# Pooled rows spread over the value blocks, weight sums on two engines, and a planner that counts a shared port

## The chip, the cores and the metric

The kernel runs on one core of one Trainium2 chip, in one launch. The metric is device time in microseconds. A run's time is that of the whole execution; a profile gives the span from the first to the last instruction, and a little time lies around it.

## The reference, cut to what matters

Eight batches, eight heads, 576 positions, 64 values a head, all in float32. Two attentions are added: one over rows averaged by fours, and one over a window of three neighbours on each side. A token mixer and a channel mixer follow, each of two matrix products with a ReLU between and a sum with its input.

```python
q_d, k_d, v_d = (t.reshape(B, H, S // 4, 4, D).mean(axis=3) for t in (q, k, v))
out_up = np.repeat(softmax(scale * q_d @ k_d.T) @ v_d, 4, axis=2)          # pooled
mask = np.abs(pos[:, None] - pos[None, :]) < 4
out_local = softmax(np.where(mask, scale * q @ k.T, -1e9)) @ v             # windowed
x = (out_up + out_local) as (B, S, H * D)                                  # 576 x 512 a batch
h = relu(x.transpose(0, 2, 1) @ w_tok1) @ w_tok2                           # 576 -> 256 -> 576
u = x + h.transpose(0, 2, 1)
out = u + relu(u @ w_ch1) @ w_ch2                                          # 512 -> 1536 -> 512
```

## The kernel before, in words

**Attention.** `load` brings queries and keys of one batch (`qk`, four tiles of 579 KB). `pool_q` sums them by fours into `qd`, on VectorE (DVE) for batches 0 and 1 and on GpSimd (POOL) later; `load_v` and `later_v` do the same for the values (`vr` into `vd`). `pooled` runs the pooled attention, one pair of heads a step: scores `sd`, maximum, exponential, transposes `td`, product `ad` with `vd`, and the scaled result `od`. `local` runs the windowed attention by tiles of four blocks of 32 queries (the last tile has two): scores `sc` against a window of `WB` keys, mask, maximum, exponential and scaling in the tile `P`, transposes `pT`, and the product `av` with the value blocks `vw`. A value block has, on 64 partitions for each head of a pair, one row of zeros, the 38 rows of the window and then 8 rows (39 to 46) for the pooled results of its 32 positions. So one product adds both attentions: columns 39 to 46 of `P` hold a constant pattern `rep` that repeats each pooled row four times, and column 0 holds the softmax's epsilon. `load_w` fills the window rows of `vw` with four DMAs a batch; once the last pair of `pooled` is done, two DMAs store `od` into the pooled rows, from ACT's queue in batches 0 and 1 and from SP's in the others.

**Mixers.** `mix` holds the token mixer. The channel mixer of batches 0 and 1 is plain (`first`, `second`, products `c` with the weights `CW` and `CX`). From batch 2 on it is a Strassen-like scheme of seven products (`first_blocks`, `second_blocks`, products `cx`, `cy`, `cz`, `dX`, `dY`, `dZ`), with chains of small additions in `after` on ACT, DVE and POOL. Its weights are sums of blocks of the weights. `weight_sums` makes them once, on POOL: six groups for each of the two weights (`C1`, then `C2`), each of four sums that are written as a high half and a rest (`put`). `keep` stores each result to HBM at once by SP's queue, and `fetch` loads them back as units `wa`, `wb`, `wc_*` for every batch.

**What sets the order.** Nothing is ordered by hand. Each piece of work is a generator that yields `step(engine, us, needs, ...)`, and `drive` is a list scheduler that runs while the kernel is built: it keeps a clock for each engine, takes the step that can start first, and among those within `PATIENCE` on the same engine the one that stands first in the list of streams. The instructions of a step are emitted then, and each engine and queue takes its instructions in that order. So the planned durations decide the order, and the real ones the time. `fetched` plans a DMA's landing from a clock `D` and a rate; `in_turn` lets at most three weight loads be under way. Until the first channel product, `keep_busy` fills planned idle time of PE with products of a constant tile `junk`.

Of the kernel before, what the change touches and what calls it, by code (L numbers as in the profile page):

```python
# [6 lines left out]
F32 = mybir.dt.float32  # L7
# [13 lines left out]
WB = QB + 6  # L21
KB = 1 + WB + QB // 4
# [9 lines left out]
BIASED = range(2, 8)  # L32
HOP = 0.12
TURN = 0.1
# [5 lines left out]
def tile_ups_attention_mixer(ctx, tc, qk, vw, vr, w1, w2, c1, c2, out):  # L40
# [15 lines left out]
    def open_pool(k, name, side):  # L56
        if k in opened:
# [6 lines left out]
    HOME = dict(cw="B", h="B", SG="B", h7="B", f="B", uh0="A", uh1="A", wy="A", ra="A", rb="A", uh="A")  # L64
    psum = ctx.enter_context(tc.tile_pool(name="psum", bufs=1, space=bass.MemoryType.PSUM))
    BUFS = dict(cw=6, h=5, xh=3, x=4, u=8, uh0=4, uh1=4, qk=4, qd=1, vw=1, vd=1, pt=2, od=1, sm=12, ev=8, sc=24,
                SG=6, wy=4, ra=3, rb=3, uh=7, h7=6)
# [28 lines left out]
    junk = pools["B"].tile([128, 512], BF16, name="junk")  # L96
# [23 lines left out]
    for p in PT:  # L120
        nc.vector.memset(p, 0.0)
        nc.vector.memset(p[:, :, 0:1], EPS)
        nc.vector.tensor_copy(p[:, :, 1 + WB:KB], rep.unsqueeze(1).to_broadcast([128, H, QB // 4]))

# [15 lines left out]
    clock = dict(A=2.0, G=5.0, V=2.0, P=0.0, S=0.0, D=0.0, R=0.0)  # L140
# [5 lines left out]
    def step(engine, us, *needs, at=None, take="", give="", mode=None):  # L146
        return engine, us, needs, at, take.split(), give.split(), mode
# [6 lines left out]

    def fetched(nbytes, rate=350e3):
        clock["D"] = max(clock["D"], now[0]) + nbytes / rate
        return clock["D"] + 1.7

    def keep_busy(n):

        if n:
            ps = P1("busy")
            for _ in range(n):
                nc.tensor.matmul(ps, junk[:, :128], junk, start=True, stop=True)

    def drive(streams):
# [3 lines left out]
        while True:  # L170
# [4 lines left out]
            for it in items:  # L175
                e, us, needs, at, take, give, m = it[1]
                if not may(it[1]) or any(not free[k.split('>')[0]] for k in take):
                    continue
                t = max([clock[e], it[2] if at is None else at] + [made[n] for n in needs]
                        + [min(free[k.split('>')[0]].values()) for k in take])  # L180
                some.append((t + (TURN if e == "P" and m != mode else 0.0), t, it))
# [3 lines left out]
            e, us, _, _, take, give, m = it[1]  # L185
# [10 lines left out]
            clock[e] = t + us  # L196
            it[2] = t + us + HOP
# [8 lines left out]
    def to_f32(raw, at, y=None, *needs):  # L206
# [9 lines left out]
        e = yield step("V", 0.08 + n * 0.0012, *needs)  # L216
# [20 lines left out]
    def token_weight(i, n, f):  # L237
        yield step("A", 0.0, ("W", "raw", i))
        raw = made["W", "raw"][i]
        if i < len(TILES):  # L240
            y = WY[i] = T([f.shape[0], n], F32, "SG", f"W1_y{i}")
        else:
            y = WY[i]
# [4 lines left out]
    def token_split(i, n, f):  # L248
        yield step("A", 0.1 + n * 0.0011, ("W", "y", i), ("t1", 0, i) if i < len(TILES) else ("mixed", 0))
        nc.scalar.copy(f[:, 0], WY[i])  # L250
        e = yield step("V", 0.08 + n * 0.0012)
# [15 lines left out]
    class Channel:  # L267
# [31 lines left out]
        def parts(self, i):  # L299
# [4 lines left out]
            t = yield step("V", 0.75)  # L304
# [102 lines left out]
    def load_v(st):  # L407
# [17 lines left out]
        for i in range(8):  # L425
# [4 lines left out]
            e = yield step("G", 1.25, at=arrives[i])  # L430
            nc.gpsimd.tensor_add(t[:, 0:2], t[:, 0:2], t[:, 2:4])
            nc.gpsimd.tensor_add(st.vd[:, g, 2 * pr:2 * pr + 2, :D], t[:, 0].rearrange("p (h d) -> p h d", d=D),
# [3 lines left out]
    def later_v(st, g):  # L436
# [5 lines left out]
        for pr in range(4):  # L442
# [4 lines left out]
            e = yield step("G", 1.3, at=fetched(147e3, 230e3), give="w")  # L447
            nc.gpsimd.tensor_add(t[:, 0:2], t[:, 0:2], t[:, 2:4])
            nc.gpsimd.tensor_add(st.vd[:, g, 2 * pr:2 * pr + 2, :D], t[:, 0].rearrange("p (h d) -> p h d", d=D),
# [3 lines left out]
    def load_w(st):  # L453
        st.vw = T([128, HG, 2, 256], F32, "vw", f"vw{st.b}")
        for lo_, hi_ in ((0, 5), (5, HG)):
            for par in range(2):
                nc.sync.dma_start(st.vw[64 * par:64 * par + 1 + WB, lo_:hi_].rearrange("p g h c -> p (g h c)"),
                                  vw[st.b, par, :, 512 * lo_:512 * hi_])
        make(("vw", st.b), fetched(1.4e6, 152e3))

    def pool_q(st, hp):
        wide = st.b < 2
        e = yield step("V" if wide else "G", 1.62 if wide else 2.9, at=st.at[hp])
        if hp == 0:
            st.qd = T([128, 4, 2, Sd], F32, "qd", f"qd{st.b}")
# [3 lines left out]
        if wide:  # L469
            for h in range(2):  # L470
                o = st.qd[:, hp, 0, G * h:G * h + G].rearrange("p (r g) -> p r g", g=HG)
                nc.vector.tensor_reduce(o, q[:, h], axis=AX.X, op=ALU.add)
            nc.vector.tensor_reduce(st.qd[:, hp, 1], k, axis=AX.X, op=ALU.add)
        else:
            o = st.qd[:, hp, 0].rearrange("p (h r g) -> p h r g", h=2, g=HG)
            for to, x in ((o, [q[:, :, :, :, f] for f in range(4)]), (st.qd[:, hp, 1], [k[:, :, f] for f in range(4)])):
                nc.gpsimd.tensor_add(to, x[0], x[1])  # L477
                nc.gpsimd.tensor_add(to, to, x[2])
                nc.gpsimd.tensor_add(to, to, x[3])
# [5 lines left out]
    def pooled(st, pr):  # L485
# [60 lines left out]
        if pr == 3:  # L546
            e = yield step("A" if b < 2 else "S", 0.2, ("vw", b), *(("pair", b, i) for i in range(3)), at=e)
            for par in range(2):
                (nc.scalar if b < 2 else nc.sync).dma_start(
                    st.vw[64 * par + 1 + WB:64 * par + KB].rearrange("p g h c -> p g (h c)"),  # L550
# [3 lines left out]
    def local(st, t):  # L554
# [18 lines left out]
        w = pp[:n, :, 1:1 + WB]  # L573
        mask = masks[0 if t == 0 else 2 if t == len(TILES) - 1 else 1]
        yield step("V", 1.48, give="gg")
        nc.vector.tensor_tensor(w.rearrange("p (hp two) k -> p two hp k", two=2),
                                ps[:n, :, :4 * WB].rearrange("p two (hp k) -> p two hp k", hp=4),
                                mask[:n].unsqueeze(1).unsqueeze(1).to_broadcast([n, 2, 4, WB]), ALU.add)
        mx = T([n, H], F32, "sm", f"mx{b}_{t}")
        nc.vector.tensor_reduce(mx, w, axis=AX.X, op=ALU.max)  # L580
        nc.vector.tensor_tensor(w, w, mx.unsqueeze(2).to_broadcast([n, H, WB]), ALU.subtract)
        yield step("A", 0.47)
        nc.scalar.activation(w, w, AF.Exp, scale=0.125)
        yield step("V", 1.16)
# [3 lines left out]
        nc.vector.tensor_tensor(w, w, r.unsqueeze(2).to_broadcast([n, H, WB]), ALU.mult)  # L588
# [13 lines left out]
        for hp in range(4):  # L602
            for j in range(nb):
                h, g = divmod(TILES[t][j], HG)
                for par in range(2):
                    p = slice(64 * par, 64 * par + KB)
# [25 lines left out]
    def mix(st):  # L632
# [8 lines left out]
        def splits():  # L641
            for t in range(NT if b else 0):
# [4 lines left out]
                e = yield step("V", 0.75)  # L647
# [89 lines left out]
        def scaled():  # L737
            for ch in range(2):
# [8 lines left out]
                for c in range(4):  # L747
# [3 lines left out]
                    e = yield step("V", 0.5)  # L751
# [4 lines left out]
        def combined():  # L756
# [9 lines left out]
            def split(name):  # L766
# [4 lines left out]
                e = yield step("V", 1.0)  # L771
                for k in range(2):
                    nc.vector.scalar_tensor_tensor(t[:, k, 1], block[name][k], s, t[:, k, 0], ALU.mult, ALU.subtract)
                make(("uh", b, name), e)

            def less(x, y, name, into=None):
# [3 lines left out]
                for k in range(2):  # L780
                    e = yield step("V", 0.5, at=0.0 if k else None, take="" if into or b == 2 else f"f>{name}{k}_{b}")
# [107 lines left out]
    def weight_sums():  # L889

        add, sub = ALU.add, ALU.subtract
        t = pools["B"].tile([128, 2, 256], F32, name="S_sum")
        eng = nc.gpsimd

        def keep(C, p, name, x):
            if C is C1:
                to, i = {"A11": (A_UNITS, 0), "S1": (A_UNITS, 1), "S2": (A_UNITS, 2), "S4": (A_UNITS, 3),
                         "A12": (B_UNITS, 0), "S3": (B_UNITS, 1), "A22": (B_UNITS, 2)}[name]
                nc.sync.dma_start(to[p][:, i], x)
            else:  # L900
                for o in range(2):
                    nc.sync.dma_start(C_UNITS[o][name][:, p], x[:, o] if name[0] == "S" else x[:, :, 128 * o:128 * o + 128])

        def put(C, p, name, x):
            yield step("G", 0.5)
            if C is C1:
                out_ = T([128, 2, 256], F16, "SG", f"{name}_{p}")
                hi, lo = out_[:, 0], out_[:, 1]
            else:
                out_ = T([128, 2, 2, 128], F16, "SG", f"{name}_{p}")  # L910
                hi, lo = out_[:, :, 0], out_[:, :, 1]
                x = x.rearrange("p (o n) -> p o n", o=2)
            if C is C2 and name == "S1":
                eng.tensor_scalar(hi, x, -1.0, None, ALU.mult)
                yield step("G", 1.2)
                eng.tensor_tensor(lo, x, hi, add)
                eng.tensor_scalar(lo, lo, -1.0, None, ALU.mult)
            else:
                eng.tensor_copy(hi, x)
                yield step("G", 0.75)  # L920
# [419 lines left out]
```

## Time and profile before

| | us |
|---|---|
| median of three runs (lowest to highest) | 928.46 (927.17 to 929.52) |
| profiled execution, its own time | 928.45 |
| its span | 926.7 |
| PE busy (share of the span) | 858.6 (93%) |
| PE weight loads busy | 679.7 (73%) |
| DVE busy | 617.0 (67%) |
| ACT busy | 410.5 (44%) |
| POOL busy | 463.2 (50%) |

PE is TensorE's products and PEld its weight loads, which run beside them; DVE is VectorE, ACT ScalarE, POOL GpSimd, and SP the engine from whose queue nearly all DMAs are issued (SPq and ACTq mark issues). `L607` is line 607 of the kernel. `out<-in` names tiles without buffer numbers, and a shape like `47*32 47x64` is that of a product. In a timeline each row has a start, a duration, the instructions that were merged (`x4`), and in brackets the idle time of the engine before them with what ended it. That last name is inferred: where the engine it names had long been done, something else ended the wait.

### The profile page before, as it was taken

The numbers are of one execution on the slowest core, as the hardware profiler recorded it, in microseconds if no ns is written. First come the engines' busy times: TensorE is split into PE (matmuls) and PEld (weight loads), VectorE is DVE, ScalarE is ACT, GpSimd is POOL, SyncE is SP. The second block draws the span as 40 slices with busy tenths as digits, with TensorE's granted clock in tenths as the row PEclk, the third lists the DMA queues.
The fourth block names the chain that finished last, engine by engine and source line by source line (L and its number), as shares of the span: only waits on it lengthen the run. The fifth ranks groups of instructions, "written<-read, shape, count | busy, mean of one in ns | idle before, by whom it ended". The sixth has DMA issues, their size and how long they took to land. (4 is left out here: it accounts for less than half of the span.)

```text
span 926.7 us, 26502 instructions
## 1 busy us (share of the span) xinstructions
PE 858.6 (93%) x11020; PEld 679.7 (73%) x11024; DVE 617.0 (67%) x1347; ACT 410.5 (44%) x958; POOL 463.2 (50%) x676
## 2 busy tenths in 40 slices
PE   8498997999599999999989999899998999999998
PEld 4355776788478877878768786778767787787776
DVE  7758996447433757688477775778475885765662
ACT  3256552324233436554365435554254544652540
POOL 6227899789969914950197205850077401330340
PEclk9889999899899999999999999999999999999999
DMA  8885336633354318544774367644565445336653
GB/s 246 223 289 191 109 95 152 200 85 87 77 172 105 95 54 290 155 148 144 216 197 139 104 168 247 162 133 129 160 216 131 145 152 145 112 103 210 200 171 120
DMA packets 71015, 145.43 MB, mean 157 GB/s; under 512 B 16720, under 2 KB 32592, under 8 KB 69648
## 3 DMA queue, kind: packets, MB, share of 16 engines
q1 hardware_dynamic: 70576, 143.16, 51.1%
q8 instruction: 86, 1.41, 0.6%
q10 hardware_dynamic: 320, 0.59, 0.3%
q14 instruction: 33, 0.27, 0.1%
HBM read 120.91 MB, written 20.45 MB: 153 GB/s over the span
## 5 line engine op out<-in xcount | busy, mean ns | idle before, releaser
L1060 POOL TENSOR_TENSOR h<-t,h 128x288 f16<-128x288 f32 x108 | 83.2, 776 | 185.8 <-ACT h L1049 175.9
L987 PEld LDWEIGHTS <-wa 128*128 128x128 f16 x864 | 81.9, 98 | 30.0 <-issue 7.8
L1148 PEld LDWEIGHTS <-wc_S 128*128 128x128 f16 x864 | 84.2, 99 | 22.0
L127 PE MATMUL c<-uh,CW 128*128 128x288 f16 x576 | 77.0, 289 | 1.4 <-DVE h L851 1.1
L987 PEld LDWEIGHTS <-wb 128*128 128x128 f16 x648 | 62.3, 98 | 19.5 <-issue 3.3
L127 PE MATMUL c<-h,CX 128*128 128x288 f16 x576 | 75.5, 287 | 0.0
L1148 PEld LDWEIGHTS <-wc_A 128*128 128x128 f16 x648 | 62.6, 98 | 16.4 <-issue 0.8
L127 PE MATMUL t<-xh,W 128*128 128x512 f32 x210 | 60.7, 422 | 11.5 <-DVE xh L648 8.7
L477 POOL TENSOR_TENSOR qd<-qk 128x144 f32<-128x144 f32 x48 | 30.9, 644 | 76.0 <-DMA qk<-in_qk_dram 76.0
L127 PEld LDWEIGHTS <-CW 128*128 128x128 f16 x576 | 55.6, 99 | 16.9 <-issue 2.5
L127 PEld LDWEIGHTS <-CX 128*128 128x128 f16 x576 | 55.0, 98 | 14.9 <-issue 1.1
L987 PE MATMUL cx<-uh_T,wb 128*128 128x288 f16 x432 | 64.8, 286 | 1.1 <-DVE y L1091 1.1
L1148 PE MATMUL dX<-h,wc_S 128*128 128x288 f16 x432 | 59.6, 294 | 0.0
L127 PE MATMUL t<-W,hid 128*128 128x288 f32 x336 | 58.4, 309 | 0.0
L1049 ACT ACTIVATE h<-t 128x288 f16<-128x288 f32 x108 | 47.9, 443 | 22.6 <-DVE t L1064 22.5
L607 PE MATMUL av<-vw,pt 47*32 47x64 f32 x2304 | 34.5, 241 | 25.0 <-DMA vw<-od 14.5
L1148 PE MATMUL dY<-h,wc_S 128*128 128x288 f16 x432 | 56.9, 286 | 0.0
L1148 PE MATMUL dX<-h,wc_A 128*128 128x288 f16 x432 | 56.6, 286 | 0.0
L127 PEld LDWEIGHTS t<-xh,W 128*128 128x128 f32 x210 | 38.1, 192 | 23.4 <-DVE xh L648 12.0
L607 PEld LDWEIGHTS av<-vw,pt 47*32 47x32 f32 x2304 | 28.1, 113 | 34.3 <-issue 24.0
L770 ACT ACTIVATE uh_T<-T,us 128x288 f16<-128x288 f32 x48 | 23.8, 529 | 59.5 <-DVE T L784 59.5
L648 DVE TENSOR_TENSOR xh<-x,xh 128x512 fp32r<-128x512 f32 x28 | 21.5, 774 | 41.0 <-ACT xh L646 40.9
(191 smaller groups left out, 2034.2 us busy)
## 6 DMA issues: line engine op xcount, KB each, us to landing
qk<-in_qk_dram SPq DMA_DIRECT2D x32, 579.0 KB
wa<-d1a SPq DMA_DIRECT2D x36, 512.0 KB
wc_S<-d_S SPq DMA_DIRECT2D x48, 384.0 KB
wb<-d1b SPq DMA_DIRECT2D x36, 384.0 KB
wc_A<-d_A SPq DMA_DIRECT2D x36, 384.0 KB
vr<-in_vr_dram SPq DMA_DIRECT2D x64, 144.0 KB
C_raw<-in_c_dram SPq DMA_DIRECT2D x16, 512.0 KB
out_dram<-u SPq DMA_DIRECT2D x24, 288.0 KB
```

Source lines behind the costliest of these rows:

```text
L127: nc.tensor.matmul(ps, lhs(a), rhs(c), start=first and i == 0, stop=last and i == 2, **kw)
L477: nc.gpsimd.tensor_add(to, x[0], x[1])
L607: nc.tensor.matmul(ps[QB * j:QB * j + QB, par, D * hp:D * hp + D], pt[p, hp, QB * j:QB * j + QB], st.vw[p, g, h, D * hp:D * hp + D], start ...
L648: nc.vector.tensor_tensor(xh[:, 1], xf(t), xh[:, 0].bitcast(F32), ALU.subtract)
L770: nc.scalar.activation(t[:, k, 0], block[name][k], AF.Copy, scale=s)
L987: nc.tensor.matmul(ps, w[:, a, 128 * k:128 * k + 128], uh[x][:, k, c], start=first_ and k == j == 0, stop=k == 1 and j == 2, skip_group_ch ...
L1049: nc.scalar.activation(here().h[:, PARTS.index(name), 0], x, f)
L1060: nc.gpsimd.tensor_tensor(h[:, i, 1], getattr(here(), x), h[:, i, 0], ALU.subtract)
L1148: nc.tensor.matmul(ps, w[:, k, a], H[k][:, i, c], start=first_ and k == j == 0, stop=k == 5 and j == 2, skip_group_check=True)
```

## The change

It has these parts:

- The window is 40 keys wide instead of 38. A value block is now loaded whole, 64 partitions for each head, in two DMAs a batch instead of four. The pooled rows lie at partitions 3, 10, 17, ... 52 of a block, with five window rows between each two. `P` has the matching columns in groups of seven, and the softmax operations work on 8 x 5 columns of a head.
- `od` is stored from SP's queue in all batches.
- `weight_sums` exists twice, once for POOL and once for DVE; each takes the next group that nobody has. On DVE, the high halves are made by ACT. The stores are steps of their own (`stores`) that become due 3 us (POOL) or 1.5 us (DVE) after the planned time of the last operation. The results have three buffers on POOL and two on DVE instead of six.
- The planner has one more clock, `X`, for a port that two-input operations of DVE and all operations of POOL take; a POOL step holds it for 0.6 of its time. Many planned durations are refined, long steps are split, and SP's clock waits for the eighth last landing. Stores of results (`results`) are planned steps of SP.
- The junk products are 192 columns wide instead of 512, and 8/3 times as many.

```diff
-WB = QB + 6
-KB = 1 + WB + QB // 4
+WB = QB + 8
+HELD = 0.6
...
     for p in PT:
         nc.vector.memset(p, 0.0)
-        nc.vector.memset(p[:, :, 0:1], EPS)
-        nc.vector.tensor_copy(p[:, :, 1 + WB:KB], rep...)
+        nc.vector.memset(p[:, :, 9:10], EPS)
+        nc.vector.tensor_copy(p[:, :, 3:53:7], rep...)
...
     def fetched(nbytes, rate=350e3):
+        if len(landed) >= 8:
+            clock["S"] = max(clock["S"], landed[-8])
         clock["D"] = max(clock["D"], now[0]) + nbytes / rate
-        return clock["D"] + 1.7
+        landed.append(clock["D"] + 1.7)
+        return landed[-1]
...
-                t = max([clock[e], it[2] if at is None else at] + ...
+                t = max([clock[e], clock["X"] if port else 0.0, it[2] if at is None else at] + ...
...
             clock[e] = t + us
+            if port:
+                clock["X"] = t + us * (HELD if e == "G" else 1.0)
...
         for lo_, hi_ in ((0, 5), (5, HG)):
-            for par in range(2):
-                nc.sync.dma_start(st.vw[64 * par:64 * par + 1 + WB, lo_:hi_]..., vw[st.b, par, :, 512 * lo_:512 * hi_])
-        make(("vw", st.b), fetched(1.4e6, 152e3))
+            nc.sync.dma_start(st.vw[:, lo_:hi_]..., vw[st.b, :, 512 * lo_:512 * hi_])
+        make(("vw", st.b), fetched(2.4e6, 330e3))
...
-            e = yield step("A" if b < 2 else "S", 0.2, ("vw", b), *(("pair", b, i) for i in range(3)), at=e)
+            e = yield step("S", 0.2, ("vw", b), *(("pair", b, i) for i in range(3)), at=e)
             for par in range(2):
-                (nc.scalar if b < 2 else nc.sync).dma_start(
-                    st.vw[64 * par + 1 + WB:64 * par + KB]...,
+                nc.sync.dma_start(
+                    st.vw[64 * par + 3:64 * par + 53:7]...,
                     st.od[:, par]...)
...
-        w = pp[:n, :, 1:1 + WB]
+        cols = pp[:n, :, 4:60].rearrange("p h (j k) -> p h j k", k=7)
+        w = cols[:, :, :, :5]
...
-        nc.vector.tensor_reduce(r, pp[:n, :, 0:1 + WB], axis=AX.X, op=ALU.add)
+        nc.vector.tensor_reduce(r, cols[:, :, :, :6], axis=AX.XY, op=ALU.add)
...
+    def stores():
+        done = {"C1": [], "C2": []}
+        n = {"G": 0, "V": 0}
+        for k in range(14 * len(FIRSTS)):
+            yield step("S", 0.1, ("store", k))
+            C, p, name, x, e = kept[k]
...
+            if name[0] == "S":
+                make(("stored", e, n[e]), end)
+                n[e] += 1
...
-    def weight_sums():
+    def weight_sums(e):
+        eng = dict(G=nc.gpsimd, V=nc.vector)[e]
+        wide, narrow = dict(G=(1.25, 0.8), V=(0.83, 0.5))[e]
+        def keep(C, p, name, x, late=0.0):
+            made["store", len(kept)] = now[0] + late
+            kept.append((C, p, name, x, e))
         def put(C, p, name, x):
-            yield step("G", 0.5)
+            yield step(e if e == "G" else "A", ..., *([("stored", e, count[0] - BUFS["S" + e])] if ... else []))
...
+            if e == "V":
+                nc.scalar.activation(hi, x, AF.Copy, scale=-1.0 if back else 1.0)
...
+        while to_sum:
+            C, p = to_sum[0]
+            f = FIRSTS[p]
+            yield step("R", 0.0, ("t1", 0, len(TILES) - 1), (C.name, f), (C.name, f + 2))
+            if (C, p) not in to_sum:
+                continue
+            to_sum.remove((C, p))
...
...
-            streams = [fetch()] + streams + [weight_sums()]
+            streams = [fetch()] + streams + [stores(), weight_sums("G"), weight_sums("V")]
```

In `after`, `mix` and `split` the steps of DVE change from 0.5 to 0.46 or 0.47 and those with two inputs in SBUF get `port=True`.

More of the change, by code (lines that the diff above doesn't have):

```diff
@@ L32 @@
 BIASED = range(2, 8)
+ON_POOL = range(2, 8)
 HOP = 0.12
+HELD = 0.6
 TURN = 0.1
@@ L175, in drive @@
             for it in items:
-                e, us, needs, at, take, give, m = it[1]
+                e, us, needs, at, take, give, m, port = it[1]
                 if not may(it[1]) or any(not free[k.split('>')[0]] for k in take):
                     continue
-                t = max([clock[e], it[2] if at is None else at] + [made[n] for n in needs]
+                t = max([clock[e], clock["X"] if port else 0.0, it[2] if at is None else at] + [made[n] for n in needs]
                         + [min(free[k.split('>')[0]].values()) for k in take])
@@ L780, in less @@
                 for k in range(2):
-                    e = yield step("V", 0.5, at=0.0 if k else None, take="" if into or b == 2 else f"f>{name}{k}_{b}")
+                    e = yield step("V", 0.46, at=0.0 if k else None, port=True, take="" if into or b == 2 else f"f>{name}{k}_{b}")
                     if not into:
@@ L899, in keep @@
                 nc.sync.dma_start(to[p][:, i], x)
+                end = fetched(131e3, 200e3)
             else:
@@ L1075, in s_chain @@
             hi("B11", p.s, AF.Relu)
-            e = yield step("V", 0.5, ("r12", b, n), take=f"f>t1{k}")
+            e = yield step("V", 0.47, ("r12", b, n), port=True, take=f"f>t1{k}")
             p.t1 = F("t1")
@@ L1094, in y_chain @@
             hi("B22", p.y, AF.Relu)
-            e = yield step("V", 0.5, ("got", "t1", b, n), take=f"f>t2{k}")
+            e = yield step("V", 0.47, ("got", "t1", b, n), port=True, take=f"f>t2{k}")
             p.t2 = F("t2")
@@ L1165, in second_blocks, with results @@
                 make(("done", b, o, name), e)
+    def results(b):
+        for o in range(2):
+            for name, h in (("A12", 0), ("A22", 1)):
+                yield step("S", 0.1, ("into", b, o, name))
+                c = o + 2 * h
+                nc.sync.dma_start(out[b, 128 * c:128 * c + 128], ready[b].u[c])
+                e = fetched(295e3, 250e3)
+            make(("over", b, o), e)
     def after_second(b):
@@ L1199, in second_weights @@
     def second_weights():
-        yield step("S", 0.0, *(("C1", "read", i) for i in range(NF)))
+        yield step("R", 0.0, *(("C1", "read", i) for i in range(NF)))
         C2.place = pairs("CX") + singles(2, "CY", pools["B"])
@@ L1205, in lazily @@
     def lazily(what, *needs):
-        yield step("S", 0.0, *needs)
+        yield step("R", 0.0, *needs)
         yield from what()
@@ L1276, in tile_ups_attention_mixer @@
         for b in range(2, B):
-            streams = sum((after(b, n) for n in range(len(FIRSTS))), [lazily(lambda b=b: after_second(b), ("done", b, 0, "A11"))]) + streams
+            streams = sum((after(b, n) for n in range(len(FIRSTS))), [lazily(lambda b=b: after_second(b), ("done", b, 0, "A11")), results(b)]) + streams
             ok = ("loaded", b)
```

205 lines of the change are left out of this document (104 added, 101 removed).

## The prediction

> **What bounds the kernel now.** I read the page first, then busy time by stage, the waits of PE, and the timelines around PE's longest waits.
>
> ```profile
> span 926.7 us, 26502 instructions
> ...
> PE 858.6 (93%) x11020; PEld 679.7 (73%) x11024; DVE 617.0 (67%) x1347; ACT 410.5 (44%) x958; POOL 463.2 (50%) x676
> ```
>
> PE is the bound on the whole: 68.1 us of the span are not PE's. The profiled execution took 928.45 us, 1.75 around its span, and the median shown is 928.46, so the sum below starts from 928.45. The next rows say where the 68 us lie (columns: stretch, its length, busy us of PE, weight loads, DVE, ACT, POOL, granted clock, DMA share, GB/s).
>
> ```profile
> 0.00:60.00 60.00, 41.90 (x767) 25.53 (x771) 38.69 (x95) 20.79 (x41) 28.14 (x60) 0.89 0.86 251
> 60.00:100.00 40.00, 36.06 (x262) 24.71 (x262) 34.62 (x75) 28.11 (x58) 24.27 (x30) 0.96 0.56 186
> 100.00:140.00 40.00, 38.28 (x463) 30.26 (x463) 38.93 (x80) 19.86 (x39) 35.03 (x45) 1.00 0.35 110
> 140.00:330.00 190.00, 173.73 (x2583) 142.16 (x2581) 100.19 (x224) 62.01 (x138) 158.52 (x237) 0.95 0.45 122
> 330.00:660.00 330.00, 316.43 (x4143) 255.48 (x4143) 238.58 (x518) 161.12 (x392) 135.93 (x195) 0.99 0.54 163
> 660.00:926.70 266.70, 252.24 (x2811) 201.55 (x2809) 165.98 (x359) 118.63 (x292) 81.27 (x112) 0.99 0.50 156
> ```
>
> The first 60 us are loads (DMA share 0.86) and PE idles 18.1. From 60 to 140 VectorE is nearly full: it has 6.5 of 80 us left. From 140 to 330 GpSimd is the fullest helper (158.5 of 190, mostly the weight sums) and PE idles 16.3. In the remaining 596.7 us PE idles 28.0, or 4.7%. GpSimd's load costs nothing by itself; what counts is which PE wait it ends in. The longest waits of PE (total, times, longest):
>
> ```profile
> PE av L607 <- DMA vw<-od: 14.5, 4, 7.9
> PE t L127 <- DVE xh L648: 8.7, 8, 2.5
> PE av L607 <- DVE CW L217: 6.2, 1, 6.2
> PE td L523 <- ACT pd L507: 4.9, 4, 1.4
> ```
>
> The first and third are one thing: the windowed products `av` wait for the pooled rows (`od`) to be stored into the value blocks `vw`. It happens in batches 0, 1 and 2.
>
> **The change part by part.** *Late stores: batch 2.* The queue SP takes its DMAs in program order and stands at the first that isn't ready.
>
> ```profile
> 239.26 0.42 DVE L543 TENSOR_TENSOR od<-ad,rd 72x256 f32<-72x256 f32 x1
> ...
> 244.41 0.85 POOL L917 TENSOR_SCALAR S<-S 128x256 f16<-128x256 f16 x1
> ...
> 245.29 0.81 SPq L902 DMA_DIRECT2D d_S<-S  x2
> ...
> 246.19 1.56 SPq L549 DMA_DIRECT2D vw<-od  x2
> ...
> 251.17 0.39 PE L607 MATMUL av<-vw,pt 47*32 47x64 f32 x2 [7.93 <-DMA vw<-od]
> ...
> 253.04 2.03 PE L607 MATMUL av<-vw,pt 47*32 47x64 f32 x126 [1.48 <-DMA vw<-od]
> ```
>
> `od` is ready at 239.68, but its two DMAs go out at 246.19, behind a store of `S` that waits for GpSimd until 245.26. They land 4.98 and 6.85 us after the first issue, while PE stands 7.93 + 1.48 = 9.41 us. That this is the queue's habit:
>
> ```profile
> SPq L899 <- POOL S L921: 79.1, 22, 12.2
> ```
>
> With stores as steps of their own, planned 1.5 or 3 us late, SP should be free at 239.8. Landings as now would then be at 244.8 and 246.65; PE comes free at 243.24 and still waits 1.55 and some 1.5, so 6.4 are saved. Pooled rows on 8 spread partitions may land sooner. Ends: 0 (something else stands before it) and -9.4; I take **-7**, near the row.
>
> [...]
>
> *`od` moved from ACT's queue to SP's: batches 0 and 1.* Batch 1:
>
> ```profile
> 144.78 1.57 SPq L457 DMA_DIRECT2D vw<-in_vw_dram  x4
> ...
> 153.88 0.42 DVE L543 TENSOR_TENSOR od<-ad,rd 72x256 f32<-72x256 f32 x1
> 154.22 1.45 POOL L919 CAST S<-S_sum 128x256 f16<-128x256 f32 x1
> 154.22 1.18 DVE L252 TENSOR_TENSOR W<-W_y,W 128x288 fp32r<-128x288 f32 x3
> ...
> 156.82 2.13 ACTq L549 DMA_DIRECT2D vw<-od  x2
> ...
> 158.51 0.40 POOL L919 CAST S<-S_sum 128x256 f16<-128x256 f32 x1
> ...
> 159.00 0.59 ACT L597 COPY pt<-pT 128x512 f32<-128x512 f32 x1 [8.46 <-POOL S L919]
> ...
> 159.64 1.11 PE L593 MATMUL pT<-ident,P 128*128 128x128 f32 x4 [3.09 <-ACT pt L597]
> ...
> 163.86 1.17 PE L607 MATMUL av<-vw,pt 47*32 47x64 f32 x62 [1.94 <-DMA vw<-od]
> ```
>
> ACT is idle 8.46 us until its copy at 159.00: behind it in program order stands no GpSimd work, but two DMA issues that could not go before 156.82, 2.5 us after `od`. The likely holder is the `vw` load issued at 144.78. On SP they no longer hold ACT, and the 3.09 us wait for `pt` can go. Against that, the load becomes whole: 128 rows of 18.4 KB (2.36 MB) in two DMAs for 78 rows (1.44 MB) in four. If 12.0 us (144.78 to 156.82) grew with the bytes it would be 19.7, and PE would lose 7.7; more rows also spread over more engines, which may cost nothing. Behind the two DMAs on SP stand this stage's stores, which nobody needs before 330. Ends -5 (3.09 + 1.94) and +7.7; I take **-2**, since most of the 3.09 is ACT's own hold.
>
> Batch 0:
>
> ```profile
> 16.61 1.78 SPq L457 DMA_DIRECT2D vw<-in_vw_dram  x4
> 18.44 15.43 SPq L233 DMA_DIRECT2D C_raw<-in_c_dram  x6
> ...
> 33.53 0.42 DVE L543 TENSOR_TENSOR od<-ad,rd 72x256 f32<-72x256 f32 x1
> 33.98 2.00 ACTq L549 DMA_DIRECT2D vw<-od  x2
> ...
> 41.49 0.39 PE L607 MATMUL av<-vw,pt 47*32 47x64 f32 x2 [6.16 <-DVE CW L217]
> ...
> 45.01 1.97 PE L607 MATMUL av<-vw,pt 47*32 47x64 f32 x121 [3.14 <-DMA vw<-od]
> ```
>
> The rows land 7.5 and 11.0 us after 33.98, against 4.98 and 6.85 in batch 2; PE stands 6.16 + 3.14 = 9.3 us. On SP, `od` is issued between weight loads and queues behind up to three (15.43 us for six issues). The larger `vw` load adds 0.92 MB at 251 GB/s, 3.7 us at most, to a stretch that the loads fill. Ends -9.3 and +5.7 (3.7 and some 2 of SP's order); I take **+1**. `vw` loads of later batches are issued as soon as the previous batch's `av` is done, and the previous batch's long products cover them.
>
> *The planner's port and costs.* This reorders everything. It can pay where VectorE or GpSimd run late against the plan and PE waits for them (xh and pd above).
>
> ```profile
> L569 PE MATMUL sc<-qk 64*32 64x38 f32 x2304 | 28.6, 206 | 1.2 <-DVE P L576 0.9 <-DVE pd L513 0.3
> ...
> L1064 DVE SCALAR_TENSOR_TENSOR u<-y,u 128x288 f32<-128x288 f32 x36 | 25.3, 702 | 0.0
> ...
> L648 DVE TENSOR_TENSOR xh<-x,xh 128x512 fp32r<-128x512 f32 x28 | 21.5, 774 | 41.0 <-ACT xh L646 40.9
> ...
> L1064 DVE SCALAR_TENSOR_TENSOR t<-cx,t 128x288 f32<-128x288 f32 x36 | 16.4, 454 | 20.4 <-ACT h L1049 14.1 <-POOL vd L449 2.3 <-POOL h L1060 1.7
> ```
>
> The same form takes 454 ns with one input in PSUM and 702 with both in SBUF; the old plan has 0.5 for both. The lengthening stays, but the plan will know of it. Ends: -14 (half of the 28.0 idle after 330) and +6 (a few new waits of the old sizes, 1.4 to 2.5 us). I take **-6**, nearer the middle, since the largest waits recur once a batch and are thus faults of the plan.
>
> *Wider windows.* `sc` has 40 columns for 38: 28.6 x 2/38 = **+1.5** on PE; 47 to 64 rows in `av` leave its columns alone. Mask, maximum and scaling grow by 5%, the sum from 312 to 384 elements; they are VectorE's, beside PE after 140. Smaller junk products fill the same time: 0.
>
> *Weight sums on two engines.* A group is 2 wide and 10 narrow two-input operations: on VectorE 2 x 0.774 + 10 x 0.454 = 6.1 us and four casts on ACT. Six of twelve groups would be 37 us. From 140 to 330 VectorE is idle 89.8 us, so there they are covered; before 140 they aren't. GpSimd gets as much lighter, but PE doesn't wait for sums, and by the code the sums are fetched back only after batch 1's first half. Fewer buffers (3 and 2 for 6) can hold VectorE's cast on ACT until a store has landed. Ends 0 and +18; I take **+1.5**.
>
> Sum: -7 - 2 + 1 - 6 + 1.5 + 1.5 = -11: **917.5 us**.
>
> **The rivals.** *VectorE becomes the bound from 60 to 140 (slower).* The sums are always ready, so a planner that takes the earliest step puts them in every hole of VectorE. If four of the six groups of the first weight fall before 140, 24.4 us meet 6.5 free, and PE loses 17.9 for the 1.5: 934. It decides from about 3.1 groups on (6.5 + 1.5 + 11 = 19 us). For it: 38.93 of 40 busy. Against: sums stand last in the list, and GpSimd's relief shortens the two-input operations. The two rows of 154.22 bear on it: a cast of 0.40 took 1.45 beside three subtractions with two SBUF inputs. [...]
>
> *The pooled rows stay late (no change).* Another DMA on SP, above all a waiting weight load or a larger `vw` load, takes the place of the stores: without the 7 and the 2 it is 926.5, and 928 if the larger load costs 1.5 more. For it: six weight loads hold SP 15 us in batch 0.
>
> *Batch 0 gains too (faster).* If spread rows land as in batch 2 or sooner, most of the 9.3 us go, 8 with them: 928.45 - 11 - 1 - 8 = 908.5. For it: from 60 to 100 PE idles only 3.9 of 40 us, so work that begins earlier can end earlier. Against: the queue.
>
> *A new order with new waits (slower).* The reordering costs +6 and batch 0 +5.7: 917.5 + 12 + 4.7 = 934.
>
> **How the numbers follow.** Forecast 0.52, batch 0 too 0.20, late rows 0.12, VectorE bound 0.11, new waits 0.05. Faster by over 0.3% (2.8 us, about what a measurement can tell) 0.72, within 0.12, slower 0.16. The predicted time is the forecast's 917.5, its own range 910 to 925. The range of 8 in 10 goes from 903, which leaves 0.1 to the ends of several gains at once, to 931, which leaves out the two slower cases at 934.
>
> **What would show it.** Right: batch 2's `od` issued within 1 us of its last VectorE operation, and its wait below 4 us; SP's waits for `S` far below 79.1; no 8 us hole of ACT near 155; PE idle after 330 near 22; fewer than three groups of sums on VectorE before 140, and PE there as full as now. Wrong: VectorE full past 140 with PE waiting for `h` or `uh`; `od` of batch 0 landing more than 11 us after it is ready; waits for xh or pd as long as now or longer.

## The result, and the profile after

The change takes 898.2 us (median of four runs, 893.67 to 899.88) where the kernel before takes 928.99 beside it (927.17 to 932.11): a ratio of 0.9658, 95% interval [0.9612, 0.9703]. Forecast were 917.5 and 903 to 931: the sign was right, and the gain is more than twice the one forecast. The profiled execution took 899.88 us, 28.57 less than the one before. Medians here and below are of executions in the chip's faster state; only the run with one engine for the sums had others, two of ten.

From the head of the page after, whose span is 897.9 us:

```profile
PE 857.5 (95%) x11112; PEld 691.5 (77%) x11112; DVE 634.4 (71%) x1410; ACT 418.9 (47%) x978; POOL 395.1 (44%) x593
```

PE is as busy as before (857.5 for 858.6), so of the 28.8 us by which the span is shorter 27.7 are idle time of PE (68.1 to 40.4). To see where, the span is cut at the same points of the work in both kernels: the first channel product of batch 0, the last one of batch 1, the end of the blocks of batch 2, the end of those of batch 5, the end. Busy time by stretch, before and then after (columns as in the prediction):

```profile
0.00:89.20 89.20, 67.96 (x949) 42.56 (x954) 62.73 (x147) 41.58 (x83) 42.37 (x78) 0.90 0.81 245
89.20:346.70 257.50, 238.71 (x3258) 193.47 (x3258) 158.47 (x347) 94.84 (x203) 203.58 (x292) 0.96 0.40 111
346.70:449.30 102.60, 100.68 (x1343) 81.69 (x1342) 75.94 (x169) 51.79 (x128) 44.46 (x65) 0.98 0.58 181
449.30:771.70 322.40, 302.60 (x4026) 243.96 (x4024) 229.94 (x489) 155.41 (x378) 136.63 (x194) 0.99 0.55 165
771.70:926.70 155.00, 148.69 (x1453) 118.00 (x1451) 89.91 (x195) 66.90 (x166) 36.11 (x48) 1.00 0.47 150
```

```profile
0.00:84.50 84.50, 72.42 (x1030) 56.30 (x1031) 60.09 (x142) 41.27 (x82) 40.74 (x77) 0.84 0.70 240
84.50:336.70 252.20, 238.48 (x3268) 193.41 (x3269) 192.89 (x417) 102.46 (x224) 148.45 (x210) 0.97 0.42 135
336.70:437.80 101.10, 99.18 (x1344) 80.72 (x1342) 75.09 (x168) 52.64 (x128) 41.62 (x65) 1.00 0.59 195
437.80:741.20 303.40, 297.25 (x4025) 242.30 (x4024) 217.83 (x490) 155.37 (x378) 128.66 (x194) 1.00 0.56 184
741.20:897.90 156.70, 150.19 (x1453) 118.82 (x1451) 88.53 (x195) 67.17 (x166) 35.61 (x48) 0.98 0.47 147
```

Stretch by stretch the change is -4.7, -5.3, -1.5, **-19.0** and +1.7 us. Two thirds lie in batches 3 to 5, where no weight sum runs, no `od` is waited for and no queue was changed. There DVE spends 217.8 us on the same work for 229.9, and POOL 128.7 for 136.6. The groups of DVE by form, in 450 to 740 us, before and after, say why (count, busy us, mean ns):

```profile
L1053 DVE SCALAR_TENSOR_TENSOR h<-y,h 128x288 f16<-128x288 f32 x18 | 14.4, 801 | 0.0
L1064 DVE SCALAR_TENSOR_TENSOR u<-y,u 128x288 f32<-128x288 f32 x18 | 14.2, 786 | 0.0
L1053 DVE SCALAR_TENSOR_TENSOR h<-s,h 128x288 f16<-128x288 f32 x18 | 13.3, 738 | 0.0
L1064 DVE SCALAR_TENSOR_TENSOR t<-y,t 128x288 f32<-128x288 f32 x18 | 11.9, 660 | 3.8 <-POOL h L1060 2.9
```

```profile
L1102 DVE SCALAR_TENSOR_TENSOR u<-y,u 128x288 f32<-128x288 f32 x18 | 13.5, 751 | 0.0
...
L1091 DVE SCALAR_TENSOR_TENSOR h<-y,h 128x288 f16<-128x288 f32 x18 | 10.2, 566 | 0.0
L1091 DVE SCALAR_TENSOR_TENSOR h<-s,h 128x288 f16<-128x288 f32 x18 | 10.1, 559 | 0.0
L1102 DVE SCALAR_TENSOR_TENSOR t<-y,t 128x288 f32<-128x288 f32 x18 | 10.0, 556 | 0.4
```

These are operations with both inputs in SBUF. They did not only come to be planned at their real length: three of the four groups became shorter, `h<-y,h` by 235 ns. The fourth, `u<-y,u`, hardly did; over the whole run its mean is 702 ns before and after. The starts and ends in the two traces show why: in batches 3 to 5, 66 of the 72 operations of these four groups run beside an operation of POOL before, and 40 after. Those that run beside none take 448 and 447 ns on average, the others 774 and 737. Of the 18 `u<-y,u`, 16 and then still 15 run beside POOL.

PE gains by this through its waits for DVE. In batches 3 to 5 the longest of them, before and after:

```profile
PE t L127 <- DVE xh L648: 7.9, 6, 2.5
```

```profile
PE t L128 <- DVE xh L660: 1.8, 1, 1.8
```

In all, PE's idle time there falls from 19.8 to 6.2 us. The other 5.4 of the 19.0 us are busy time of the same products. The granted clock was 0.99 before and 1.00 after, which by itself would make some 3 us of that (an estimate, 1% of 302.6).

The waits of PE and of SP's queue, after:

```profile
PE av L619 <- DMA vw<-od: 7.6, 5, 3.1
PE td L531 <- ACT pd L515: 7.5, 5, 3.2
PE sd L503 <- DVE pd L521: 3.1, 1, 3.1
```

```profile
SPq L912 <- POOL S L955: 23.0, 6, 7.5
...
SPq L916 <- DVE S L955: 15.4, 6, 5.4
```

The wait for `od` has halved, 14.5 to 7.6, the 6.2 for `CW` in front of `av` is gone, and the single largest wait of SP for a sum is 7.5 for 12.2. In batch 2 all goes as forecast:

```profile
236.21 0.42 DVE L551 TENSOR_TENSOR od<-ad,rd 72x256 f32<-72x256 f32 x1
236.66 1.44 SPq L557 DMA_DIRECT2D vw<-od  x2
...
238.20 1.83 SPq L916 DMA_DIRECT2D d_S<-S  x4
...
240.82 0.84 PE L619 MATMUL av<-vw,pt 64*32 64x64 f32 x62 [0.91 <-DMA vw<-od]
```

`od` is ready at 236.63 and issued at 236.66; the stores of `S` stand behind it, and PE waits 0.91 us for 9.41.

### The profile page after: what moved, and what is told of

Read it like the earlier page. It is cut to its first block, busy times and chain, and to the rows that moved or that the text cites. A ratio compares the mean times of both kernels' runs of the same rounds, so it can differ in the third digit from the quotient of the medians.

```text
span 897.9 us, 26687 instructions
## 1 busy us (share of the span) xinstructions
PE 857.5 (95%) x11112; PEld 691.5 (77%) x11112; DVE 634.4 (71%) x1410; ACT 418.9 (47%) x978; POOL 395.1 (44%) x593
## 4 chain that ended last, share of the span: by engine, by line
PE 81%; DVE 9%; DMA 4%; ACT 2%; POOL 2%; issue 2%; SPq 1%; ACTq 0%; DVEq 0%; POOLq 0%
PE dX L1186 12%; PE c L128 11%; PE t L128 11%; PE cx L1025 10%; PE dY L1186 6%; PE cy L1025 6%; PE ad L541 3%; PE cz L1025 3%; PE dZ L1186 3%; PE av L619 3%; PE sc L577 2%; PE pT L605 2%; PE td L531 2%; PE sd L503 2%; PE t L690 2%
## 5 line engine op out<-in xcount | busy, mean ns | idle before, releaser
L128 PE MATMUL c<-uh,CW 128*128 128x288 f16 x576 | 75.2, 286 | 0.4 <-issue 0.4
L457 POOL TENSOR_TENSOR vr<-vr 72x256 f32<-72x256 f32 x48 | 37.0, 770 | 60.3 <-DMA vr<-in_vr_dram 51.2
L128 PE MATMUL t<-xh,W 128*128 128x512 f32 x210 | 58.8, 414 | 4.7 <-DVE xh L660 2.5
L487 POOL TENSOR_TENSOR qd<-qd,qk 128x144 f32<-128x144 f32 x96 | 60.6, 631 | 6.3
L1186 PE MATMUL dX<-h,wc_S 128*128 128x288 f16 x432 | 56.9, 286 | 0.0
L1087 ACT ACTIVATE h<-t 128x288 f16<-128x288 f32 x108 | 47.6, 442 | 12.6 <-DVE t L1102 12.5
L1227 DVE SCALAR_TENSOR_TENSOR u<-dX,io,u 128x288 f32<-128x288 f32 x48 | 24.8, 517 | 34.0 <-PE dX L1186 33.7
L128 PEld LDWEIGHTS t<-W,hid 128*128 128x128 f32 x336 | 46.6, 189 | 0.0
```

Source lines behind the costliest of these rows:

```text
L128: nc.tensor.matmul(ps, lhs(a), rhs(c), start=first and i == 0, stop=last and i == 2, **kw)
L487: nc.gpsimd.tensor_add(to, to if f > 1 else x[0], x[f])
L1087: nc.scalar.activation(here().h[:, PARTS.index(name), 0], x, f)
L1186: nc.tensor.matmul(ps, w[:, k, a], H[k][:, i, c], start=first_ and k == j == 0, stop=k == 5 and j == 2, skip_group_check=True)
L1227: nc.vector.scalar_tensor_tensor(u, blocks_[b, o, name], io, u, ALU.mult, ALU.add)
```

## The experiments

The theory to begin with (A): the planner's count of the port, with its new costs, carries the gain. (The port is a term of the plan, the clock `X`: the traces show how long operations take beside POOL and apart from it, 774 and 448 ns above, and no port.) Its rival (B): the moved work does it (rows, stores, queue, a second engine for the sums). Each expectation says what A and B stand for in that run.

**Leave out the count.** The changed kernel with one term of the planner removed:

```diff
-                t = max([clock[e], clock["X"] if port else 0.0, it[2] if at is None else at] + ...
+                t = max([clock[e], it[2] if at is None else at] + ...
```

> The changed kernel, but the planner no longer waits for the port clock X; durations, split steps, sums on two engines, late stores and the new rows stay. Theory A (the planner's port keeps VectorE's two-input operations and GpSimd apart, and that is most of the 19 us gained in batches 3 to 5): those batches go from about 101 back to 105 to 107 us each, the operations h<-y and h<-s from about 560 ns back above 650, and the time rises by 10 to 20 us to 908 to 918. Rival B (finer steps and truer durations do it): within 4 us of 898. Rival C (the planned order of SP's DMAs does it): within 4 us of 898.

Measured: 922.7 us, ratio to before 0.9924 [0.9893, 0.9955]. The count carries more than A had foreseen: without it 24.5 of the 30.8 us are gone. Batches 3 to 5 take 320.9 us, nearly the 322.4 of before, and three of the four groups are long again in this run (`u<-y,u` has 700 ns, less than in the changed kernel); 59 of the 72 operations run beside POOL:

```profile
441.60:762.50 320.90, 305.68 (x4026) 245.04 (x4024) 229.25 (x489) 155.66 (x378) 134.21 (x194) 0.98 0.55 174
```

```profile
L1102 DVE SCALAR_TENSOR_TENSOR t<-y,t 128x288 f32<-128x288 f32 x18 | 12.3, 681 | 1.0
L1091 DVE SCALAR_TENSOR_TENSOR h<-s,h 128x288 f16<-128x288 f32 x18 | 12.1, 671 | 0.0
L1091 DVE SCALAR_TENSOR_TENSOR h<-y,h 128x288 f16<-128x288 f32 x18 | 12.1, 670 | 0.0
```

Of the 17.5 us that batches 3 to 5 take longer than in the changed kernel, 9.1 are idle time of PE and 8.4 busy time, at a granted clock of 0.98 for 1.00. Whether the lower clock comes from the waits is not shown.

**Do the count alone.** The kernel before, with the clock `X`, the split steps and the new durations, all else as it was; and the same without the term above, so that only the split steps and the durations are new.

```diff
-            e = yield step("V", 0.5, ("r12", b, n), take=f"f>t1{k}")
+            e = yield step("V", 0.47, ("r12", b, n), take=f"f>t1{k}", port=True)
...
+            if port:
+                clock["X"] = t + us * (HELD if e == "G" else 1.0)
```

> The kernel before, with only the planner's port, the split steps and the new durations for attention, splits and chains; rows, sums on GpSimd, stores and queues as before. Theory A or B: batches 3 to 5 take about 101 us each instead of 106 to 110, and the time falls by 12 to 20 us to 909 to 917; the wait for od in batch 2 (9.4 us) stays, give or take its reordering. Rival C: batches 3 to 5 as before, time within 5 us of 928.

> As the one above, but the planner doesn't count the port: only split steps and new durations. Theory A: little or nothing, 922 to 932, h<-y still above 700 ns in batches 3 to 5. Rival B: as the one above, 909 to 917.

Measured: 929.37 with the count (0.9995 [0.9966, 1.0025]) and 920.56 without it (0.9866 [0.9822, 0.9911]). So theory A falls: the count alone gains nothing, and the durations and split steps alone, which A had put at little or nothing, gain 1.3%. Batches 3 to 5 in the run with the count and then in the one without:

```profile
464.10:772.10 308.00, 298.61 (x4026) 243.29 (x4024) 216.46 (x489) 156.30 (x378) 127.77 (x194) 0.99 0.60 172
```

```profile
448.60:759.70 311.10, 301.21 (x4024) 243.29 (x4023) 220.79 (x489) 155.37 (x378) 134.62 (x194) 0.99 0.59 171
```

Both are shorter than the 322.4 of before. The count does to the overlaps what it does in the changed kernel: 41 of the 72 operations run beside POOL with it and 60 without. But here that is worth 3.1 us in these batches, and 11.3 of the 14.4 come with the durations and split steps, against A's sign of `h<-y` above 700 ns (662 here). In the changed kernel the same term is worth 17.5 us. Each figure is from one profiled execution, and why they differ so much stays open.

The gain of the run with the count is lost again in one place, ahead of batch 2: the stretch of batch 2's blocks takes 122.6 us for 102.6. The timeline of this run:

```profile
350.75 0.67 POOL L929 TENSOR_TENSOR S<-S_sum,S 128x256 f16<-128x256 f32 x1
...
358.87 0.40 ACT L1078 COPY s<-cx 128x288 f32<-128x288 f32 x1 [12.80 <-DMA d_S<-S]
...
359.32 1.60 PE L995 MATMUL cx<-uh_T,wa 128*128 128x288 f16 x6 [14.37 <-ACT s L1078]
```

PE stands 14.37 us at the start of batch 2's blocks for ACT's first copy `s`, and that copy for the last stores of `S`. By the code, `s` lies in the pool "hidden", which is opened in the memory of the second weight and of its sums and so has to wait for the last store. With the port counted, POOL's additions are put off, and the last sum comes at 350.75. Without it (the second run) they end at 331, and no wait of PE is above 1.3 us from there to 460.

**One engine for the sums.** The changed kernel with `weight_sums("V")` taken out of the streams:

```diff
-            streams = [fetch()] + streams + [stores(), weight_sums("G"), weight_sums("V")]
+            streams = [fetch()] + streams + [stores(), weight_sums("G")]
```

> The changed kernel with all weight sums on GpSimd. If the second engine for the sums brings something, it is before 330 us: theory D (sums on VectorE relieve GpSimd where batch 0 and 1 wait for it) loses 3 to 8 us, 901 to 906; the prediction's term of +1.5 says 896 to 898 or no difference. Batches 3 to 5 stay at 101 us by either.

Measured: 923.9 (0.9937 [0.99, 0.9975]), 26 us above the changed kernel and far outside what was expected. The same wait stands in its timeline:

```profile
360.99 0.67 POOL L955 TENSOR_TENSOR S<-SG_sum,S 128x256 f16<-128x256 f32 x1
361.48 0.40 ACT L1108 COPY s<-cx 128x288 f32<-128x288 f32 x1 [11.41 <-DMA d_S<-S]
361.93 1.60 PE L1025 MATMUL cx<-uh_T,wa 128*128 128x288 f16 x6 [13.52 <-ACT s L1108]
```

Besides, PE waits 22.3 us for `od` in this run, for 7.6 in the changed kernel. So the new theory (A from here on): the count pays only if the sums end before batch 2 needs their memory, and for that they need a second engine. The next two runs test it from both sides.

**The count and the second engine, on the kernel before.** The kernel with the count (929.37), and `weight_sums` and `stores` as in the change; rows, windows, and the queue of `od` as before. (The junk products are the narrow ones, since the extra buffers need their space.)

> The kernel before, with the planner that counts the port and the new durations, and with the weight sums on two engines and their late stores; pooled rows, windows and queues of od as before. Theory A (planning the port pays as soon as the sums end early enough to free the memory that batch 2 needs): sums end near 312, no wait of PE above 4 us at the start of batch 2's blocks, batches 3 to 5 near 305 together, and 902 to 910. Theory B (the gain needs the new rows and queues): 915 or more.

Measured: 903.63 (0.9713 [0.967, 0.9756]): the second engine takes 25.7 us off a kernel in which the count alone did nothing, inside A's range. No wait of PE above 1.7 us stands at the start of batch 2's blocks or after it.

**All sums on POOL, but less of them.** This kernel is for timing alone: in each group it leaves out four narrow additions of ten, and in every second group the two wide ones, so it is not a complete kernel.

```diff
-            yield step(e, narrow, at=0.0, port=True)
-            eng.tensor_tensor(t[:, 1], t[:, 1], a11[:, 1], sub)
...
-            yield step(e, wide, at=0.0, port=True)
-            eng.tensor_tensor(t, a11, a21, sub)
+            if p % 2 == 0:
+                yield step(e, wide, at=0.0, port=True)
+                eng.tensor_tensor(t, a11, a21, sub)
```

> The changed kernel with all weight sums on GpSimd, and only part of each sum computed (four narrow additions of ten and, in half of the groups, both wide ones are left out), so that GpSimd has some 97 us of them. Theory A (the sums on one engine cost 27 us only because they end at 362 and hold the memory that batch 2 needs): they end near 310, the 13.5 us wait is gone and the time is 894 to 904. Theory B (VectorE's share matters for another reason, such as the order that it gives to the plan): 910 or more although the sums end early.

Measured: 893.71 (0.9612 [0.9565, 0.9658]). With POOL's load lighter and nothing on DVE, the loss is gone, so no second engine is needed if the sums end early. Against the profile with all sums on POOL, 18.6 us go in the stretch of batch 2's blocks (119.3 to 100.7), where the 13.52 us wait stood. Another 14.0 go before it (262.6 to 248.6), where PE also waits less for `od` (10.5 for 22.3); how much of that is the early end and how much the lighter load is not told apart. When the last of their stores to the second weight's units were issued (first and last start of the group `d_S<-S`), in the changed kernel and in this one:

```profile
L916 SPq DMA_DIRECT2D d_S<-S x48: 319/422/1742, 207.3 to 311.4; - x48
```

```profile
L916 SPq DMA_DIRECT2D d_S<-S x48: 319/417/1990, 203.9 to 298.9; - x48
```

**A longer hold in the plan.** `HELD = 1.0` for 0.6:

> The changed kernel, but the planner holds the port for the whole of an instruction of GpSimd instead of 0.6 of it. Theory A (both engines lose as long as their instructions overlap at all): the operations of VectorE with two inputs in SBUF get shorter still (t<-y,t and u<-y,u from 588 and 702 ns towards 500), batches 3 to 5 take as long or 1 to 3 us less, and the time is 892 to 899. Theory B (GpSimd needs the port only part of the time, and a longer hold makes the plan put work off that could run): operations as now, batches 3 to 5 longer by 1 to 5 us, 898 to 906.

Measured: 927.54 (0.9993 [0.9962, 1.0023]), a loss that neither had foreseen in its size, and in the main the same place once more: batch 2's blocks take 118.0 us for 101.1, and the stretch before them 260.3 for 252.2. Its stores and its waits:

```profile
L916 SPq DMA_DIRECT2D d_S<-S x48: 319/423/1352, 248.6 to 359.6; - x48
```

```profile
PE av L619 <- DMA vw<-od: 17.0, 5, 8.0
PE cx L1025 <- ACT s L1108: 12.6, 1, 12.6
```

Here two engines share the sums, but the plan puts them off until 357. Over all runs: where the last of these stores is issued after 350 us (357.9, 359.6, 362.1) PE loses 12.6 to 14.4 us at that point; where it is issued by 332, none. Whether 0.6 or 1.0 is the better hold can't be read from this run: `u<-y,u` is shorter (599 ns for 702), `h<-y,h` longer (655 for 562), and batches 3 to 5 take 306.4.

**The rows together.** The changed kernel with the pooled rows on neighbouring partitions:

```diff
...
-                    st.vw[64 * par + 3:64 * par + 53:7].rearrange("p g h c -> p (g h c)"),
+                    st.vw[64 * par + 44:64 * par + 52].rearrange("p g h c -> p (g h c)"),
...
```

> The changed kernel, but the pooled rows lie on eight neighbouring partitions (44 to 51 and 108 to 115) instead of every seventh. Theory A (the spread makes the landing shorter): from issue to landing the two od DMAs take about 2 us longer than in the changed kernel, PE waits 1 to 2 us more for them in batches 0, 1 and 2, and the time is 900 to 904. Theory B (the time of a landing is not set by where the rows lie): landings as in the changed kernel and 897 to 900.

Measured: 904.09 (0.9718 [0.9673, 0.9763]), at the upper edge of theory A's range. Batch 2 in its timeline:

```profile
239.05 1.45 SPq L557 DMA_DIRECT2D vw<-od  x2
...
243.93 0.30 PE L619 MATMUL av<-vw,pt 64*32 64x64 f32 x2 [1.68 <-DMA vw<-od]
245.88 1.17 PE L619 MATMUL av<-vw,pt 64*32 64x64 f32 x62 [1.66 <-DMA vw<-od]
```

The rows land 4.88 and 6.83 us after the first issue, as in the kernel before (4.98 and 6.85). Spread, with the same issue, PE goes on after at most 2.96 and after 4.16: 1.9 and 2.7 us sooner. In batch 0 it is 3.87 and 5.07 us for 5.54 and 7.14. PE's wait for `od` is 18.1 us for 7.6: 5.6 more in batch 0 and 2.4 in each of batches 1 and 2, above the 1 to 2 of theory A.

**The queue of `od`.** The changed kernel with `od` of batches 0 and 1 on ACT's queue again:

```diff
-            e = yield step("S", 0.2, ("vw", b), ...
+            e = yield step("A" if b < 2 else "S", 0.2, ("vw", b), ...
```

> The changed kernel, but batches 0 and 1 issue od again from ACT's queue. Theory A (the move to SP is worth something of its own): ACT stands behind the issue in batch 1 as before the change (a hole near 8 us, PE waiting some 3 us for pt) and the loss is 2 to 8 us: 900 to 906. Theory B (what was gained in batches 0 and 1 comes from the plan, not from the queue): 896 to 900, and the batch-0 wait for od stays near 4 us.

Measured: 895.09 (0.9616 [0.9578, 0.9654]): the move to SP brings no time that can be seen (the intervals of the two ratios overlap). Batch 1 here and then in the changed kernel:

```profile
149.80 0.42 SPq L466 DMA_DIRECT2D vw<-in_vw_dram  x1
...
151.65 0.42 DVE L551 TENSOR_TENSOR od<-ad,rd 72x256 f32<-72x256 f32 x1
...
158.82 2.04 ACTq L557 DMA_DIRECT2D vw<-od  x2
...
166.15 0.39 PE L619 MATMUL av<-vw,pt 64*32 64x64 f32 x2 [4.40 <-issue]
```

```profile
156.12 1.00 SPq L466 DMA_DIRECT2D vw<-in_vw_dram  x2
...
158.60 0.42 DVE L551 TENSOR_TENSOR od<-ad,rd 72x256 f32<-72x256 f32 x1
...
168.42 1.46 SPq L557 DMA_DIRECT2D vw<-od  x2
...
171.81 0.27 PE L619 MATMUL av<-vw,pt 64*32 64x64 f32 x2 [2.44 <-DMA vw<-od]
```

On either queue `od` is ready 6.8 to 9.4 us before it is issued, and the issue comes 9.0 and 12.3 us after the rows of the `vw` load shown here. For the kernel before that was 12.0. If it is the load that holds `od`, which is inferred here as in the prediction, the one of 2.36 MB holds it no longer than the one of 1.44 did. Theory A's effect is there in part: on ACT's queue PE goes on 7.3 us after the issue and stands 4.40 us, and ACT stands 4.9; on SP's queue PE goes on after 3.4 us and stands 2.44. But it does not show in the time.

**A better number for the landing.** The plan takes 2.5 us for the landing of `od`, and it lasts 3.9 to 5.1 in batch 0. Two kernels with 5.0, on the changed kernel and on the one with ACT's queue, beside the changed kernel itself:

```diff
-            make(("full", b), e, 2.5)
+            make(("full", b), e, 5.0)
```

> The changed kernel once more, as the yardstick for the three kernels that run beside it: 893 to 900 by both theories.

> The changed kernel, but the planner takes 5.0 us instead of 2.5 for the landing of od. Theory A (PE waits for od because the plan takes the landing for shorter than the 3.9 to 5.1 us that it lasts, and there is other work for PE in batches 1 and 2): the waits of av for od in batches 1 and 2 (3.7 and 1 us) go, and the time is 2 to 5 us below the changed kernel beside it. Theory B (there is nothing else that PE could do then, and the wait only gets another name): within 1.5 us of it, with as much idle time of PE from 130 to 340.

> The changed kernel with od on ACT's queue in batches 0 and 1 and 5.0 us planned for its landing. Theory A (both edits gain, by different waits): 889 to 894 and 3 to 8 us below the changed kernel beside it. Theory B (od on ACT's queue was not faster by itself; the 895 seen for it lay within what any other order of the plan gives): within 2.5 us of the changed kernel.

Measured: the changed kernel 896.98 (895.64 to 899.32; ratio 0.9647 [0.9611, 0.9682]), with 5.0 us 892.8 (890.43 to 896.95; 0.9609 [0.9566, 0.9653]), and with ACT's queue as well 901.58 (899.32 to 904.23; 0.9696 [0.966, 0.9732]). The first gains 4.2 us on the changed kernel, as A had it; the intervals of the two ratios still overlap. It has the lowest ratio of the complete kernels, but the 0.9616 with ACT's queue can't be told from it. PE's waits before `av` in batches 1 and 2 are down to 0.6 and 0.5 us. That of batch 0 stands under another name, as it did before the change:

```profile
PE av L619 <- DVE CW L225: 5.4, 1, 5.4
```

The second falls outside both expectations. Two edits, neither of which lost by itself, cost 4.6 us together. The plan takes another order from batch 0's second channel products on: half of the products with `CX` are done at 178.7 us for 205.1, but all of them at 340.9 for 333.7. Why that order is worse is left open. It shows what an edit of this planner's numbers can move by itself: some 5 us either way. What is said above of the rows and of the queue rests on the traces, then, and not on differences of time of that size.

## Why the prediction was wrong, step by step

The sum was -11; the profiled execution has -28.57. By the stretches above, which add up to the 28.8 of the span, the start (forecast +1) gave -4.7, batches 0 to 2 from there on -6.8, and everything later (forecast -6) -17.3.

- *Late stores in batch 2, -7.* Right: 8.5 us of wait went (9.41 to 0.91), and SP issues `od` 0.03 us after it is ready. With the rows together 6.1 went (3.34 us of wait are left), near the 6.4 worked out for landings as before; the spread rows brought the rest. That spread rows may land sooner was the author's guess, with no row of before behind it; with the rows spread PE goes on 1.9 and 2.7 us sooner after the issue than with them together, and why is not shown.
- *`od` on SP's queue, -2.* The waits in batch 1 fell from 5.03 to 2.79 (2.44 and 0.35), so the size is right, but not for the reason given. The run with ACT's queue has no loss in time, and the 9.4 us between ready and issue in batch 1 remain on SP. The landing of spread rows shortened these waits (with the rows together they are 5.23); what the new order did to them is not told apart. The larger load, priced up to +7.7, cost nothing that can be seen: from the `vw` load's issue to that of `od` in batch 1 the 16 DMA engines had a mean busy share of 0.79 and moved 176 GB/s before (12.0 us), and 1.03 and 385 GB/s after (12.3 us).
- *Batch 0, +1.* Wrong sign: the rival "batch 0 gains too" came true in its sign. The hold on SP came as feared (`od` is ready at 35.83 and issued at 39.19), but the rows then land after 3.87 and 5.07 us, for 7.5 and 11.0, and PE stands 3.9 us for 9.3. The first channel product begins 4.7 us earlier. All variants with the new plan begin it earlier than the 89.2 of before (80.8 to 86.7), the kernel before with the new plan alone at 83.6, so the plan does it, and spread rows aren't needed for it. It repeats only within some 3 us: a second execution of the changed kernel has 81.8 for 84.5.
- *The planner's port and costs, -6.* This is the step that failed, in the sentence "The lengthening stays, but the plan will know of it". For the row shown with it, `u<-y,u`, it did stay (702 ns). For `h<-y,h`, `h<-s,h` and `t<-y,t` it did not: the count takes the operations beside POOL in these groups from 59 to 40 of 72 (run without the count, changed kernel). From before to after, 12 us of DVE's work in batches 3 to 5 vanish, and PE idles 6.2 us there for 19.8. The row that told of it was in the prediction: the cast of 0.40 us that took 1.45 beside three subtractions. It was weighed there for the rival with VectorE as the bound, and not as the price that the overlaps in batches 3 to 5 were paying (774 ns for 448). There both engines are busy for less time after the change, on the same work: DVE 217.8 us for 229.9 (490 and 489 instructions), POOL 128.7 for 136.6 (194 in both). What slows two operations that overlap is not shown. The lower end, -14, was half of PE's idle time after 330; the fall there was 13.4 us of idle time, and the same products of batches 3 to 5 were busy 5.4 us less besides. That 24.5 us hang on the count is shown; how much of the -19.0 comes by shorter operations and how much by the new order is not, since on the kernel before the durations and split steps alone gave 11.3.
- *Weight sums on two engines, +1.5.* Wrong in kind. "PE doesn't wait for sums" was read from a trace in which they end at 327, before the 346.7 at which batch 2's blocks need their memory. The count of the port itself pushes them to 351 and later, and then PE does wait, 13 to 14 us. With the count in place the second engine is worth 26 us (929.4 to 903.6, and 923.9 to 898.2); without it the sums are early anyway. Costing each part alone on the trace of before could not see it:

| | sums on POOL alone | sums on both engines |
|---|---|---|
| port not counted | 920.6 (rows of before) | 922.7 (new rows) |
| port counted | 929.4 (rows of before), 923.9 (new rows) | 903.6 (rows of before), 898.2 (new rows) |

- *VectorE as the bound.* Didn't happen. One operation on DVE falls before 140 us, the other sums after it, where the prediction had found DVE idle for 89.8 us.
- *Wider windows, +1.5.* About right in size: `sc` takes 29.6 us for 28.6. But `av` takes 33.2 for 34.5, and PE's busy time is 1.1 us lower in all, with other junk products and other clocks in it.

Of the signs listed, `od` in batch 2, SP's waits, the missing 8 us hole of ACT near 155 and the sums on DVE before 140 were right. (ACT now stands 6.8 us at 163.6, for the landing of a store that frees one of the two buffers: the hold that the prediction named for the smaller buffers.) PE's idle time after 330 was to be near 22 and is 14.6; that line pointed to the step at fault. Of the signs of being wrong, one half came: PE's waits for `xh` fell (8.7 to 2.5), but those for `pd` grew (4.9 to 7.5, and for `sd` 1.8 to 3.1), and still the whole is faster.

## What to carry to other kernels

When two engines slow each other down, a schedule that knows of it can remove slow times and not only plan them. So look at the difference between the contended and the free duration of every overlapping operation (here 774 and 448 ns), and at whether the engine that bounds the kernel waits for them. Putting work off has a deadline that a trace with slack doesn't show: before costing delayed work at nothing, look up who next needs its memory, and when. Where a list scheduler sets the order, test a part both alone and as the one left out; here the count gains nothing without the second engine, and all the rest of the change only 0.8% without the count.

## What was not expected of the hardware

The time to store eight rows of 18.4 KB in each of two blocks differed in these runs with the partitions they lie on: in batch 2, 4.9 and 6.8 us on eight neighbours, at most 3.0 and 4.2 on every seventh, with the same bytes and the same queue. And an overlap costs an operation of DVE with both inputs in SBUF much: over the four groups above 447 ns on average without an operation of POOL beside it, and 737 to 774 with one. POOL gains from being kept apart as well: in batches 3 to 5 its 194 instructions took 128.7 us for 136.6, and 134.2 in the run without the count.
